# Attention results in two parts, no empty TensorE instructions in the first layer, and one more joined pair of steps

## The chip, the cores and the metric

The kernel runs on one core of a Trainium2 chip. The metric is the device time of one execution in microseconds, lower is better; the median of three executions of the kernel before is 538.77 us (537.64 to 538.97). Everything is computed in fp32.

## The reference

Two parts follow each other. The first is a linear attention with a decaying state (RWKV-6), for 4 batches, 8 heads, 768 tokens and head size 48:

```python
for t in range(S):
    cur = np.einsum('bhd,bhe->bhde', u[None] * kt, vt)
    y[:, :, t] = np.einsum('bhd,bhde->bhe', rt, state + cur)
    state = wt[:, :, :, None] * state + np.einsum('bhd,bhe->bhde', kt, vt)
```

The second is a two-layer network over the 3072 tokens, each a row of 8 x 48 = 384 numbers:

```python
h = x @ w_in            # (3072, 384) x (384, 2048), the first layer
g = h - np.tanh(h)
return g @ w_out        # (3072, 2048) x (2048, 384), the second layer
```

## The kernel before

**Blocks and steps.** The tokens are cut into eight blocks of 384 (a batch has two, `q` is 0 or 1). For each block the network runs through 16 steps `f`, one for each 128 columns of `w_in`. While block `i` goes through the network, the attention of block `i + 1` is worked out between its steps, so `xT`, the transposed input of the next block, is ready when it begins. All engine orders but that of POOL are fixed by the order in which the code is written: in each step the plan (`plan`) names the attention work, `ops` lists what VectorE does and in which order, and `due` holds the second-layer products of earlier steps with the step in which TensorE gets them (`add_due`).

**First layer.** `first` (L892) makes the 128 x 384 product `hp` of one step with three matmuls of 384 columns; each fp32 matmul is two hardware instructions in the trace, so a step is six. Behind each matmul stand 0, 2 or 3 empty instructions (`NO_OP`), as the table `SPACED` says for the block and the part of it. For some pairs of steps (`JOINED`) both products are made together by a scheme with fewer multiplications (`Twos.begin`, L939 to L970): eleven matmuls of 192 columns (22 instructions, L958) into the PSUM tiles `att0` and `att1`, with sums of weights (`kept`, formed by VectorE at the places of `FORMED`) and differences of token columns (`turned`, L942), and four VectorE additions afterwards (`joint`, L968).

**Activation and second layer.** ScalarE takes `tanh` twice (L984, L985) and a square (L988), VectorE multiplies them to `g` (L902). For most blocks the second layer uses a scheme with 15 products of 128 x 128 for two steps; VectorE forms sums of `g` for it (L1007), and TensorE makes the products in two parts of six (L1088, twelve instructions each, in step `f + 2` and `f + 3` of the odd step `f`) and one of three. In a joined pair the sums of an odd step are made one step later than otherwise (`carried`).

**Attention results.** `together` (L755) makes the block's `y`, transposed, in `att0` and `att1`. For each of 8 heads and 6 chunks of 64 tokens there is one product from the states (`pre` with `states`; with `q` = 0 the first chunk has none) and one from the scores (`v` with `scores`), each 48 x 64 and small enough that four run in different quarters of the array. They come in four stretches of 48 instructions (two parts, two halves `cross` each). An empty GpSimd memset between the first and the second stretch of the same half keeps their order. With `q` = 1 the states come first, with `q` = 0 the scores. Behind them ScalarE copies the result to `xT` (L753), and small DMAs of SyncE fill its holes (L801). This happens in step 13 of blocks 0 and 1 and in step 12 of blocks 2 to 6, after the second-layer products that are due in that step. The scores of the current chunk are written into `scores` by VectorE before (`diagonal_in`, L407: one copy for pairs 2 and 3, then one for pairs 0 and 1).

Of the kernel before, what the change touches and what calls it, by code (L numbers as in the profile page):

```python
# [50 lines left out]
B, H, S, D = 4, 8, 768, 48  # L51
P = 128
L = 64
NB = 384
NQ = S // NB
NCH = NB // L
NCP = NCH // 2
# [4 lines left out]
UP = 2  # L62
HALVES = (UP, 0)
ALL = tuple(range(NPAIR))
# [15 lines left out]
LATE = 3  # L80
SPACED = (3, 0), (0, 3), (3, 2), (2, 3), (3, 2), (2, 3), (3, 0), (0, 0)

# [38 lines left out]
TWOS = range(7)  # L121
BESIDE = (1, 3, 4, 7)
JOINED = {2: (4, 7), 3: BESIDE, 4: BESIDE, 5: BESIDE, 6: BESIDE, 7: TWOS}
PAIRS = range(1, 2), range(3, 5), range(7, 8)
LEFT = range(0, 3, 2), range(5, 7)
FORMED = {(1, 8): (1, (0, 2, 1, 4, 3)), (1, 15): (0, (0, 2, 1, 4, 3)), (2, 6): (2, (0, 2, 1, 4, 3)),
          (6, 11): (3, (0, 2)), (6, 12): (4, (0, 2)), (6, 13): (3, (1, 4, 3)), (6, 14): (4, (1, 4, 3))}
# [8 lines left out]
def kernel(  # L136
# [193 lines left out]
    class Block:  # L330
# [425 lines left out]
        def together(self, ps):  # L756

            self.results(ps)
            yp, spread, St, ended = self.yp, isinstance(ps, Kept), states[self.q], {}

            def scores(p, c, h, par):
                toks = slice(64 * par, 64 * par + 64)
                return self.v[toks, c, p * D2 + h * D:p * D2 + (h + 1) * D], A[toks, h, p, c, :]

            def from_state(p, c, h, par):
                rows = slice(64 * h, 64 * h + D)
                return St[rows, p, 2 * c + par, 0:D], self.chunk("pre", p, 2 * c + par, spread)[rows]

            def stretch(of, cross):
                first = cross not in ended  # L770
                begun = set()
                for n in range(UP):
                    for c in range(NCP):
                        for h in range(2):
                            for x in range(2):
                                p, par = UP * n + x, x ^ cross
                                if of is from_state and not (self.q or c or par):
                                    continue
                                lhs, rhs = of(p, c, h, par)
                                e0, n0 = 64 * (h ^ x), (n * NCP + c) * L  # L780
                                done = nc.tensor.matmul(yp[x][e0:e0 + D, par, n0:n0 + L], lhsT=lhs, rhs=rhs,  # L781
                                                        start=first and (x, e0) not in begun, stop=True,
                                                        skip_group_check=True)
                                begun.add((x, e0))
                                if not first and len(begun) == 1:
                                    begin_behind(ended[cross], done)
                if first:
                    ended[cross] = nc.gpsimd.memset(ended_at, 0.0)
                    begin_behind(done, ended[cross])

            for of in (from_state, scores) if self.q else (scores, from_state):
                for cross in range(2):
                    stretch(of, cross)
            self.result_out(ALL, None if spread else [nc.scalar.copy] * 2)
            self.fill_holes([nc.sync])

# [95 lines left out]

    def first(xT, f, hp, apart=0):
        for kc in reversed(range(KC)):
            nc.tensor.matmul(hp, lhsT=w_in_sb[:, f, kc, :], rhs=xT[kc],  # L895
                             start=(kc == KC - 1), stop=(kc == 0))
            for _ in range(apart):
                nc.tensor.nop(nofuse=True, hint="apart")
        return hp
# [448 lines left out]
    for i, blk in enumerate(blocks):  # L1348
# [9 lines left out]
        for f in range(NF):  # L1358
# [6 lines left out]
            if not joined:  # L1365
                h = first(here, f, to[:, 0:NB], SPACED[i][f > 12 + (i < 2)])
                g, made, square, later_ops = slight(h, now, i, f)
            elif f % 2 == 0:
                for op in behind:
                    op()  # L1370
                behind = []
                outs = twos.begin(ps_a, f // 2)
                if near:
                    for name in ("split 2 0", "split 2 1", "split 0 01"):
                        later.phase(ps_a, name)
# [25 lines left out]
            if (i, f) in FORMED:  # L1401
                spare += twos.weight_forms(*FORMED[i, f])
            if later and i in JOINED and f == (i == 2) or i == blocks_n - 2 and f == 14:
                spare += twos.token_forms(xT if f > 1 else here, twos.halves((turned, 0), (turned, NB)))
# [206 lines left out]
```

## Time and profile before

| | |
|---|---|
| median of three executions | 538.77 us |
| the profiled execution's own time | 538.27 us |
| its span, first to last instruction | 536.4 us |
| mean granted TensorE clock | 0.995 |
| TensorE busy (PE) | 526.9 us, 98% |
| VectorE busy (DVE) | 462.5 us, 86% |
| ScalarE busy (ACT) | 310.3 us, 58% |
| GpSimd busy (POOL) | 9.1 us, 2% |

A row of a timeline gives the start in us from the span's start, the length, the engine, the line, the operation with the tiles it writes and reads, and how many instructions were merged. Matmuls overlap: the length of a row reaches to the end of its last instruction, and the time that a row takes from the stream is the start of the next row less its own.

### The profile page before, as it was taken

The numbers are of one execution on the slowest core, as the hardware profiler recorded it, in microseconds if no ns is written. First come the engines' busy times: TensorE is split into PE (matmuls) and PEld (weight loads), VectorE is DVE, ScalarE is ACT, GpSimd is POOL, SyncE is SP. The second block draws the span as 40 slices with busy tenths as digits, with TensorE's granted clock in tenths as the row PEclk, the third lists the DMA queues.
The fourth block names the chain that finished last, engine by engine and source line by source line (L and its number), as shares of the span: only waits on it lengthen the run. The fifth ranks groups of instructions, "written<-read, shape, count | busy, mean of one in ns | idle before, by whom it ended". The sixth has DMA issues, their size and how long they took to land.

```text
span 536.4 us, 14922 instructions
## 1 busy us (share of the span) xinstructions
PE 526.9 (98%) x5950; PEld 437.5 (82%) x5950; DVE 462.5 (86%) x970; ACT 310.3 (58%) x720; POOL 9.1 (2%) x57
## 2 busy tenths in 40 slices
PE   8899999999999999999999999999999999999996
PEld 5756666677887889889789898899888897899994
DVE  7899897699979889988998899988999889667874
ACT  4899984666445573555655475374735655435450
POOL 1100000000000000000000000000000000000001
PEclk9899999999999999999999999999999999999999
DMA  8698733252302622162313722146221510100011
GB/s 280 224 404 333 241 105 109 89 148 61 120 13 89 163 74 89 51 137 82 120 57 75 178 60 68 50 90 165 63 90 39 140 40 2 56 1 2 11 34 47
DMA packets 53046, 56.33 MB, mean 105 GB/s; under 512 B 21488, under 2 KB 50928, under 8 KB 52976
## 3 DMA queue, kind: packets, MB, share of 16 engines
q1 hardware_dynamic: 52592, 55.18, 34.2%
q8 instruction: 49, 0.80, 0.7%
q14 instruction: 21, 0.17, 0.1%
q10 hardware_dynamic: 288, 0.10, 0.1%
q0 software_dynamic: 96, 0.07, 0.1%
HBM read 44.73 MB, written 4.72 MB: 92 GB/s over the span
## 4 chain that ended last, share of the span: by engine, by line
PE 96%; DMA 1%; issue 1%; ACT 0%; DVE 0%; SPq 0%; PEldq 0%; PEld 0%; DVEq 0%
PE acc L1088 27%; PE hp L895 27%; PE att L958 17%; PE acc L1039 6%; PE att L781 4%; PE hp L1088 3%; PE att L1088 3%; PE att L504 3%; PE att L585 2%; PE acc L1066 1%; PE att L895 1%; DMA r<-in_rT 1%; PE acc L895 1%; PE att L527 1%; PE att L689 1%
## 5 line engine op out<-in xcount | busy, mean ns | idle before, releaser
L895 PE MATMUL hp<-xT,w_sb 128*128 128x384 f32 x438 | 154.3, 488 | 0.7 <-issue 0.7
L1088 PE MATMUL acc<-forms,g 128*128 128x128 f32 x972 | 135.9, 276 | 0.0
L1088 PEld LDWEIGHTS acc<-forms,g 128*128 128x128 f32 x972 | 124.0, 192 | 4.3
L895 PEld LDWEIGHTS hp<-xT,w_sb 128*128 128x128 f32 x438 | 78.6, 190 | 43.5 <-issue 0.9
L1007 DVE TENSOR_TENSOR g<-g 128x256 f32<-128x256 f32 x270 | 107.1, 419 | 4.6 <-PE acc L1088 0.3
L984 ACT ACTIVATE h<-hp 128x384 f32<-128x384 f32 x73 | 35.9, 492 | 96.8 <-PE hp L895 96.8
L902 DVE SCALAR_TENSOR_TENSOR g<-h,qa 128x384 f32<-128x384 f32 x112 | 61.7, 551 | 21.8 <-ACT h L988 21.4
L988 ACT ACTIVATE h<-h 128x384 f32<-128x384 f32 x113 | 58.7, 519 | 0.0
L1088 PE MATMUL acc<-w_sb,g 128*128 128x128 f32 x324 | 54.1, 276 | 0.0
L958 PE MATMUL att<-xT,w_sb 128*128 128x192 f32 x250 | 53.0, 326 | 0.0
L1088 PEld LDWEIGHTS acc<-w_sb,g 128*128 128x128 f32 x324 | 46.4, 192 | 5.5
L968 DVE TENSOR_TENSOR joint<-joint,att 128x384 f32<-128x384 f32 (+1 forms) x72 | 34.6, 501 | 18.0 <-PE att L958 11.0
L984 ACT ACTIVATE h<-joint 128x384 f32<-128x384 f32 x36 | 18.7, 518 | 39.7 <-DVE joint L968 39.7
L958 PEld LDWEIGHTS att<-xT,w_sb 128*128 128x128 f32 x250 | 41.4, 190 | 0.0
L985 ACT ACTIVATE qa<-hp 128x384 f32<-128x384 f32 x73 | 35.7, 489 | 0.0
L1123 DVE TENSOR_TENSOR sums<-sums 128x256 f32<-128x256 f32 x84 | 32.9, 410 | 1.4 <-ACT sums L1100 0.9
L1039 PE MATMUL acc<-w_sb,sums 128*128 128x384 f32 x96 | 33.7, 487 | 0.0
L271 ACT ACTIVATE up<-raw 128x768 f16<-128x768 f32 (+1 forms) x32 | 32.7, 1093 | 0.0
L1039 PEld LDWEIGHTS acc<-w_sb,sums 128*128 128x128 f32 x96 | 18.1, 190 | 12.3
L427 DVE TENSOR_TENSOR_SCAN pre<-w,start 128x780 f32<-128x780 f32 x14 | 25.0, 1782 | 0.8
L439 DVE TENSOR_TENSOR_SCAN post<-w,seed 128x780 f32<-128x780 f32 x14 | 24.9, 1775 | 0.0
L958 PE MATMUL att<-turned,kept 128*128 128x192 f32 x126 | 23.9, 326 | 0.0
(157 smaller groups left out, 768.3 us busy)
## 6 DMA issues: line engine op xcount, KB each, us to landing
raw<-in_weights SPq DMA_DIRECT2D x16, 768.0 KB, 6.4
w<-in_wT SPq DMA_DIRECT2D x7, 780.0 KB, 5.4
k<-in_kT SPq DMA_DIRECT2D x7, 768.0 KB, 4.5
r<-in_rT SPq DMA_DIRECT2D x7, 768.0 KB, 4.4
v_sb<-in_v SPq DMA_DIRECT2D x8, 576.0 KB, 4.1
k<-in_tokens SPq DMA_DIRECT2D x7, 576.0 KB, 4.2
r<-in_tokens SPq DMA_DIRECT2D x7, 576.0 KB, 4.9
out_y<-sums SPq DMA_DIRECT2D x18, 128.0 KB, 1.9
```

The source lines that it names most:

```text
L271: return lambda: nc.scalar.activation(out=to, in_=of, func=AF.Copy, scale=scale, bias=bias)
L895: nc.tensor.matmul(hp, lhsT=w_in_sb[:, f, kc, :], rhs=xT[kc], start=(kc == KC - 1), stop=(kc == 0))
L902: return lambda: nc.vector.scalar_tensor_tensor(out=out, in0=in0, scalar=scalar, in1=in1, op0=op0, op1=ALU.mult)
L958: nc.tensor.matmul(to, lhsT=lhs, rhs=rhs, start=n == 0, stop=n + 1 == len(of))
L968: return [lambda of=of: nc.vector.tensor_tensor(out=of[0], in0=of[1], in1=of[2], op=ALU.add) for of in ((h[:, 0:5:4], twice(h[:, 3]), both ...
L984: made = nc.scalar.activation(out=t, in_=h, func=AF.Tanh, scale=INNER / UPSCALE)
L985: nc.scalar.activation(out=by, in_=h, func=AF.Tanh, scale=OUTER / UPSCALE)
L988: nc.scalar.activation(out=t, in_=t, func=AF.Square, accum_out=top[:, n:n + 1])
L1007: return lambda: nc.vector.tensor_tensor(out=G[:, to:to + 2], in0=two(G, g_at(q, a0), g_at(q, a1)), in1=two(G, g_at(q, b0), g_at(q, b1)), ...
L1039: nc.tensor.matmul(acc, lhsT=g[:, j * P:(j + 1) * P], rhs=w_out_sb[:, f, :], start=(f == self.first), stop=(f == NF - 1))
L1088: nc.tensor.matmul(to, lhsT=G[:, g_at(q, a), :], rhs=rhs, start=start, stop=stop, skip_group_check=True)
L1123: ops.append(lambda op=op, at=at: nc.vector.tensor_tensor(out=at[0], in0=at[1], in1=at[2], op=OPS[op]))
```

## The change

Three edits stand in it. The table `SPACED` and the argument `apart` go, so `first` issues no empty instruction any more; of 516 empty instructions of TensorE 33 are left, all in the second layer of block 0. `together` is cut into `of_scores` and `of_states`, the scores always first; in the loop over steps the products that are due (`add_due`) now stand between the two. In block 2, pair 1 (steps 2 and 3) becomes a joined pair; for that the sums of weights for pair 1 are formed first (block 1, step 8), those for pairs 3 and 4 last (block 2, step 6), the token differences of block 2 are made in step 0 and not in step 1, and the early `split` of the attention's keys stays out of block 2.

```diff
-SPACED = (3, 0), (0, 3), (3, 2), (2, 3), (3, 2), (2, 3), (3, 0), (0, 0)
...
-JOINED = {2: (4, 7), 3: BESIDE, 4: BESIDE, 5: BESIDE, 6: BESIDE, 7: TWOS}
+JOINED = {2: (1, 4, 7), 3: BESIDE, 4: BESIDE, 5: BESIDE, 6: BESIDE, 7: TWOS}
...
-FORMED = {(1, 8): (1, (0, 2, 1, 4, 3)), (1, 15): (0, (0, 2, 1, 4, 3)), (2, 6): (2, (0, 2, 1, 4, 3)),
+FORMED = {(1, 8): (0, (0, 2, 1, 4, 3)), (1, 15): (2, (0, 2, 1, 4, 3)), (2, 6): (1, (0, 2, 1, 4, 3)),
...
         def together(self, ps):
 
+            self.of_scores(ps)
+            self.of_states()
+
+        def of_scores(self, ps):
+
             self.results(ps)
-            yp, spread, St, ended = self.yp, isinstance(ps, Kept), states[self.q], {}
+            self.spread, self.stretched = isinstance(ps, Kept), {}
+            for cross in range(2):
+                self.stretch(0, cross)
+
+        def of_states(self):
+            for cross in range(2):
+                self.stretch(1, cross)
+            self.result_out(ALL, None if self.spread else [nc.scalar.copy] * 2)
+            self.fill_holes([nc.sync])
...
-    def first(xT, f, hp, apart=0):
+    def first(xT, f, hp):
         for kc in reversed(range(KC)):
             nc.tensor.matmul(hp, lhsT=w_in_sb[:, f, kc, :], rhs=xT[kc],
                              start=(kc == KC - 1), stop=(kc == 0))
-            for _ in range(apart):
-                nc.tensor.nop(nofuse=True, hint="apart")
         return hp
...
-                if near:
+                if near and i > 2:
                     for name in ("split 2 0", "split 2 1", "split 0 01"):
                         later.phase(ps_a, name)
...
-            if later and i in JOINED and f == (i == 2) or i == blocks_n - 2 and f == 14:
+            if later and i in JOINED and not f or i == blocks_n - 2 and f == 14:
...
+            if later and "results" in phases.get(f, ()):
+                later.of_scores(ps_a)
             add_due(now)
             if later and "results" in phases.get(f, ()):
-                later.together(ps_a)
+                later.of_states()
```

The first place is TensorE at the results of the next block, here in step 12 of block 2. Before, the due products stand ahead of both parts:

```order
L895 MATMUL hp<-xT_1315,w_sb 128x384
L898 NO_OP x3
L1088 MATMUL acc_131<-forms,g 128x128 x4
L1088 MATMUL acc_602<-w_sb,g 128x128
L1088 MATMUL acc_602<-forms,g 128x128
L781 MATMUL att_126<-pre,states_103 48x64
L781 MATMUL att_125<-pre,states_103 48x64
```

Now the 48 matmuls with the scores (the last two are shown) stand directly behind the first layer's, then the due products, then the 48 with the states:

```order
L795 MATMUL att_126<-scores,v_sb 48x64
L795 MATMUL att_125<-scores,v_sb 48x64
L1094 MATMUL acc_131<-forms,g 128x128 x4
L1094 MATMUL acc_602<-w_sb,g 128x128
L1094 MATMUL acc_602<-forms,g 128x128
L795 MATMUL att_126<-pre,states_103 48x64
L795 MATMUL att_125<-pre,states_103 48x64
```

The scores have moved ahead of one part of six second-layer products, and one run of 96 small matmuls has become two of 48.

The second place is VectorE in steps 2 to 4 of block 2, around the new joined pair. Before (`pre<-w,start` is the scan for the next block's attention, `g<-h,qa` the activation's product, `g<-g` the sums for the second layer):

```order
L427 SCALAR_TENSOR_TENSOR pre<-w,start 128x780
L1007 TENSOR_TENSOR g<-g 128x256
L902 SCALAR_TENSOR_TENSOR g<-h,qa 128x384
L1007 TENSOR_TENSOR g<-g 128x256 x4
L426 RECIPROCAL start<-whole 128x12
```

Now, from the first of the two scans on:

```order
L426 SCALAR_TENSOR_TENSOR pre<-w,start 128x780
L974 TENSOR_TENSOR joint<-joint,att_126 128x2x192
L1013 TENSOR_TENSOR g<-g 128x256
L974 TENSOR_TENSOR joint<-joint,att_125 128x384
L974 TENSOR_TENSOR joint<-joint,att_125 128x192
L974 TENSOR_TENSOR joint<-joint,att_125 128x384
L1013 TENSOR_TENSOR g<-g 128x256
L425 RECIPROCAL start<-whole 128x12
L426 SCALAR_TENSOR_TENSOR pre<-w,start 128x780
L908 SCALAR_TENSOR_TENSOR g<-h,qa 128x384
L1013 TENSOR_TENSOR g<-g 128x256
L908 SCALAR_TENSOR_TENSOR g<-h,qa 128x384
```

Four additions have come in, and both products `g<-h,qa` of the pair now stand behind the second scan; the three sums `g<-g` of step 4, two of which TensorE reads in that step, follow the last row shown.

The third place is ScalarE in the same steps, now:

```order
L965 COPY joint<-att_126 128x192
L1106 ACTIVATE sums<-acc_602 128x512
L1106 ACTIVATE sums<-acc_131 128x512
L990 ACTIVATE h<-joint 128x384
L991 ACTIVATE qa<-joint 128x384
L994 ACTIVATE h,top<-h 128x384
L990 ACTIVATE h<-joint 128x384
L991 ACTIVATE qa<-joint 128x384
L994 ACTIVATE h,top<-h 128x384
```

Before, these activations read `hp` and not `joint`, and the first three stood ahead of the two `sums<-acc`, which wait for the last products of the block before.

More of the change, by code (lines that the diff above doesn't have):

```diff
@@ L756, in together, with stretch @@
         def together(self, ps):
+            self.of_scores(ps)
+            self.of_states()
+        def of_scores(self, ps):
             self.results(ps)
-            yp, spread, St, ended = self.yp, isinstance(ps, Kept), states[self.q], {}
+            self.spread, self.stretched = isinstance(ps, Kept), {}
[6 more added lines that the diff above has]
+            self.fill_holes([nc.sync])
+        def stretch(self, part, cross):
+            yp, spread, St, ended = self.yp, self.spread, states[self.q], self.stretched
             def scores(p, c, h, par):
@@ L767, in from_state @@
                 return St[rows, p, 2 * c + par, 0:D], self.chunk("pre", p, 2 * c + par, spread)[rows]
[L769 to L795, printed above, removed]
+            of, first, begun, last = (from_state if part else scores), cross not in ended, set(), None
+            for n in range(UP):
+                for c in range(NCP):
+                    for h in range(2):
+                        for x in range(2):
+                            p, par = UP * n + x, x ^ cross
+                            if part and not (self.q or c or par):
+                                continue
+                            lhs, rhs = of(p, c, h, par)
+                            e0, n0 = 64 * (h ^ x), (n * NCP + c) * L
+                            last = nc.tensor.matmul(yp[x][e0:e0 + D, par, n0:n0 + L], lhsT=lhs, rhs=rhs,
+                                                    start=first and (x, e0) not in begun, stop=True,
+                                                    skip_group_check=True)
+                            begun.add((x, e0))
+                            if not first and len(begun) == 1:
+                                begin_behind(ended[cross], last)
@@ L797, in fill_holes @@
+            if first:
+                ended[cross] = nc.gpsimd.memset(ended_at, 0.0)
+                begin_behind(last, ended[cross])
         def fill_holes(self, engines, which=range(2 * KC)):
@@ L1365 @@
             if not joined:
-                h = first(here, f, to[:, 0:NB], SPACED[i][f > 12 + (i < 2)])
+                h = first(here, f, to[:, 0:NB])
                 g, made, square, later_ops = slight(h, now, i, f)
```

## The prediction

> **What bounds the kernel now.** I read the page first: busy times, granted clock and the chain that ended last.
>
> ```profile
> span 536.4 us, 14922 instructions
> PE 526.9 (98%) x5950; PEld 437.5 (82%) x5950; DVE 462.5 (86%) x970; ACT 310.3 (58%) x720; POOL 9.1 (2%) x57
> PEclk9899999999999999999999999999999999999999
> PE 96%; DMA 1%; issue 1%; ACT 0%; DVE 0%; SPq 0%; PEldq 0%; PEld 0%; DVEq 0%
> ```
>
> TensorE (PE) is busy 98% of the span, the chain is PE for 96%, and its clock is full from the third slice on. Whether it ever waits for others is in the view of the waits, PE alone (us in total, times, longest):
>
> ```profile
> PE att L504 <- issue: 1.5, 1, 1.5
> PE hp L895 <- issue: 0.7, 1, 0.7
> ```
>
> Beside two short waits at the very start these are all, and both are for "issue", for nothing that another engine does. The 1.5 lies in the first 25 us, which no edit touches. So the kernel is one row of TensorE instructions without holes, and the forecast is the sum of what the change does to that row: instructions saved, changes of form added, waits that come in and the one that goes. VectorE at 86% and the ScalarE chain count where they come late.
>
> **Empty instructions.** Timeline of PE, first in block 1, where the table gives none, then in block 2, with three behind each matmul (a row's time is the next row's start less its own):
>
> ```profile
> 107.20 2.10 PE L895 MATMUL hp<-xT,w_sb 128*128 128x384 f32 x6
> 109.14 0.61 PE L1088 MATMUL acc<-w_sb,g 128*128 128x128 f32 x4
> ...
> 161.27 2.10 PE L895 MATMUL hp<-xT,w_sb 128*128 128x384 f32 x6
> 163.21 1.05 PE L1088 MATMUL acc<-forms,g 128*128 128x128 f32 x8
> ...
> 164.55 2.10 PE L895 MATMUL hp<-xT,w_sb 128*128 128x384 f32 x6
> ```
>
> A step takes 1.94 us without them and 1.94 with nine. The 483 that go were hidden behind running matmuls, and the clock was full with and without them: 0 us. (The twelve second-layer instructions after the second step take 164.55 - 163.21 = 1.34; I need that below.)
>
> **Splitting the results.** A run of small matmuls costs something at both ends. Block 2, then a small run between two large ones, with the end of a third in block 3:
>
> ```profile
> 171.10 2.10 PE L895 MATMUL hp<-xT,w_sb 128*128 128x384 f32 x6
> 173.13 1.63 PE L504 MATMUL att<-pre,post 48*64 48x64 f32 x96
> ...
> 201.52 1.05 PE L1088 MATMUL acc<-forms,g 128*128 128x128 f32 x8
> ...
> 202.95 1.56 PE L781 MATMUL att<-pre,states 48*48 48x64 f32 x96
> 204.33 1.52 PE L781 MATMUL att<-scores,v_sb 64*48 64x64 f32 x96
> 205.78 2.20 PE L895 MATMUL hp<-xT,w_sb 128*128 128x384 f32 x6
> ```
>
> ```profile
> 224.65 1.14 PE L958 MATMUL att<-xT,w_sb 128*128 128x192 f32 x6
> ...
> 228.22 1.05 PE L1088 MATMUL acc<-forms,g 128*128 128x128 f32 x8
> ...
> 230.96 2.10 PE L895 MATMUL hp<-xT,w_sb 128*128 128x384 f32 x6
> 232.99 1.63 PE L504 MATMUL att<-pre,post 48*64 48x64 f32 x96
> 234.55 1.16 PE L1088 MATMUL acc<-forms,g 128*128 128x128 f32 x8
> ...
> 235.99 1.46 PE L895 MATMUL hp<-xT,w_sb 128*128 128x384 f32 x4
> ```
>
> Going in: six of L895 ahead of small ones take 173.13 - 171.10 = 2.03 and not 1.94, so 0.09. Coming out: twelve of L1088 behind small ones take 235.99 - 234.55 = 1.44 and not 1.34, so 0.10. Inside the run there is a fixed part too, since the array fills and empties. Instructions of L781 in two stretches of that run (us, PE busy, count):
>
> ```profile
> 202.95:203.25 0.30, 0.30 (x20) 1.00 0.01 0
> 202.95:205.25 2.30, 2.30 (x164) 1.00 0.04 7
> ```
>
> 144 more in 2.00 us are 13.9 ns each; 192 would take 2.67 and took 205.78 - 202.95 = 2.83, so 0.16 is fixed. From below: the half with the way out takes 1.45, the half with the way in 1.38, at least 0.07. From above: two lone runs like L504's (234.55 - 232.99 = 1.56) would take 3.12, 0.29 more. I take 0.16, as it comes from these instructions themselves. Each split adds one run: 0.16 + 0.09 + 0.10 = 0.35 us (0.26 to 0.48). Seven blocks (0 to 6) prepare a next one: **+2.45 us** (1.8 to 3.4). The twelve second-layer instructions are only moved. Where the states came first, their sums now have more time.
>
> **Block 0: the scores are asked for too early.** Here the scores came second (q of block 1 is 1). PE, then DVE:
>
> ```profile
> 76.34 2.10 PE L1039 MATMUL acc<-w_sb,sums 128*128 128x384 f32 x6
> 78.37 1.56 PE L781 MATMUL att<-pre,states 48*48 48x64 f32 x96
> ```
>
> ```profile
> 75.15 1.95 DVE L407 COPY_PREDICATED scores<-mask_all,diagonal 128x768 f32<-128x768 uint8 x2
> ```
>
> The second of the two copies, for pairs 0 and 1, with which the stretch begins, ends at 77.10. PE would start the scores at 76.34 + 0.09 = 76.43; the due products and the states had covered that. No edit touches DVE's rows before. PE waits 77.10 - 76.43 = 0.67 and some hundredths for the release: **+0.70 us** (0.6 to 0.75). Behind the waiting matmul stand the six of L1039 and the states, so all of PE.
>
> **Pair 1 of block 2.** Two steps of 1.94 are 3.88; a joined pair is 228.22 - 224.65 = 3.57: **-0.31 us**. But with it two of the three sums for the pair before (steps 0 and 1) come a step later on DVE, behind the pair's own products. Block 3 has the same pair, and there ACT (first row) and DVE run so:
>
> ```profile
> 229.76 1.09 ACT L1100 ACTIVATE sums<-acc 128x512 f32<-128x512 f32 x2 [0.46 <-PE acc L1088]
> ```
>
> ```profile
> 228.42 1.41 DVE L968 TENSOR_TENSOR joint<-joint,att 128x384 f32<-128x384 f32 x3 [1.03 <-PE att L958]
> ...
> 233.53 0.56 DVE L902 SCALAR_TENSOR_TENSOR g<-h,qa 128x384 f32<-128x384 f32 x1 [0.22 <-ACT h L988]
> 234.00 1.09 DVE L1007 TENSOR_TENSOR g<-g 128x256 f32<-128x256 f32 x3
> 235.01 0.76 DVE L1123 TENSOR_TENSOR sums<-sums 128x256 f32<-128x256 f32 x2
> ```
>
> ```profile
> L1007 DVE TENSOR_TENSOR g<-g 128x256 f32<-128x256 f32 x270 | 107.1, 419 | 4.6 <-PE acc L1088 0.3
> L427 DVE TENSOR_TENSOR_SCAN pre<-w,start 128x780 f32<-128x780 f32 x14 | 25.0, 1782 | 0.8
> ```
>
> PE's products end, ACT takes two `sums` and six activations, DVE the product (released by ACT) and three sums `g` (0.42 each, three in 1.09), ready at 234.42, 234.76 and 235.09. PE needs the first for its third product of step 4 and the last for the fifth. In block 3 that fits, because 96 small matmuls (L504) stand ahead of these products. In block 2 they come a step later. On block 3's clock: after the pair 24 products end at 230.96, the step takes 1.94, so the products begin at 232.90 and the third is due 4 x 0.112 (1.34 / 12) later, at 233.35. It waits for 234.42 + 0.05: 1.12. The fifth is then due at 234.92 and waits for 235.14: 0.22. Together **+1.34 us**. Block 2's DVE has the second scan and its reciprocal (0.2, an estimate) there: through by 228.42 + 1.41 + 0.42 + 0.2 + 1.78 = 232.2, before the two products, so ACT stays the last. If the sums were earlier, the next would be late: DVE's `pre` for the run L504 of step 5 would be ready at 235.01 + 0.76 + 1.75 = 237.52, by this row of block 2,
>
> ```profile
> 170.83 1.75 DVE L446 TENSOR_TENSOR pre<-r,pre 128x1536 f32<-128x1536 f32 x1
> ```
>
> while PE without the first wait gets there at 232.90 + 1.34 + 2.03 = 236.27: 1.25 instead of 1.34. So 1.1 to 1.5.
>
> **The issue wait in block 6.** It stands right behind the results:
>
> ```profile
> 457.01 0.59 PE L895 MATMUL hp<-xT,w_sb 128*128 128x384 f32 x1
> 458.25 1.77 PE L895 MATMUL hp<-xT,w_sb 128*128 128x384 f32 x5 [0.66 <-issue]
> ```
>
> ```profile
> q8 instruction: 49, 0.80, 0.7%
> ```
>
> After small matmuls the first takes 0.32 + 0.10, so the next was due at 457.43 and came 0.82 late. The queue that brings instructions moved 49 packets of 0.80 MB / 49 = 16 KB; PE has 5950 + 5950 + 516 instructions, 253 a packet. The results are 384 (192 matmuls, as many loads) in 2.83 us, one and a half packets: I read the wait as the next packet's. A half is 192, less than one packet, and then come 24 in 1.34 us. So it goes: **-0.82 us** (0 if it only moves, -1.5 if untraced runs pay the longer of the two issue waits here).
>
> The Trainium skill ("Runtime: NRT & Kernel Launch", section Instruction fetch mechanics) has blocks of 16 KiB and 256 instructions, which the 49 packets agree with. It also says that a block's crossing is mostly hidden, since the sequencer, at about 20 cycles an instruction, is slower than the fill. That the trace doesn't bear out here: a small matmul and its load follow each other in 13.9 ns, and PE stood 0.82 us with no other releaser. By the page nothing would come back, and the sum would be 4.18.
>
> **Sum.** 2.45 + 0.70 + 1.34 - 0.31 - 0.82 = +3.36 us. The profiled execution took 538.27, with 1.9 around its span; that gives 541.6. The median of the runs lies 0.5 above it, which gives 542.1. I take 541.9. What a measurement of this kernel tells from no change is about 0.3%, 1.6 us.
>
> **Rivals.**
> - *The two DVE waits don't come.* PE is later by the splits, DVE has holes, and block 3 does the same pair without a wait. Against it: the chain in block 2 starts with PE's own products, and in block 0 DVE's rows follow without a hole. If DVE is 0.7 and 1.3 us earlier there: 538.77 + 2.45 - 0.31 - 0.82 = 540.1, within 0.3%.
> - *The issue wait stays or moves.* For it: the instruction addresses shift by 483, and other runs of 192 may meet a late packet. Against it: the runs of L504 (192 with their loads) had none after the start. 538.77 + 4.18 = 542.95, slower.
> - *The scores wait in blocks 2 to 6 as well.* They write the tiles that DVE's last read of the update leaves:
>
> ```profile
> 201.12 0.35 DVE L597 TENSOR_TENSOR states<-states,att 128x192 f32<-128x192 f32 x1
> ```
>
> It ends at 201.47, and PE comes at 201.52 + 0.09. If DVE is 0.3 later than I think: 5 x 0.3 more, 543.6.
> - *Instruction fetch costs far more in untraced runs.* The place is the long run in each of seven blocks, the price between the two issue waits, 0.82 and 1.5, so 5.7 to 10.5 us, all of which the split would save. In the middle: 538.77 + 4.18 - 8.1 = 534.9, faster. It decides from 5.8 us on (4.18 + 1.6). Against it: the traced run paid 0.82 and took only 0.5 less than the median.
>
> **How the numbers follow.** My forecast 0.66; waits don't come 0.12; issue wait stays 0.10; more waits 0.05; fetch 0.07. Slower 0.66 + 0.10 + 0.05 = 0.81, same 0.12, faster 0.07. The likeliest's own range, from the terms' bounds: 1.8 + 0.6 + 1.1 - 0.31 - 1.5 = 1.7 to 3.4 + 0.75 + 1.5 - 0.31 = 5.3 at the extremes; all at one end at once is unlikely, so +2.3 to +4.6, 540.8 to 543.1. The range takes in the stayed wait and most of the first rival: 539.7 to 543.3.
>
> **What would show it.** The split: seven pairs of small runs, each 1.49 or so, with 2.03 before and 1.44 after. Block 0: a PE wait of 0.7 at the scores, released by DVE's `scores`. Block 2: waits of 1.1 and 0.2 in step 4's products, released by `g`. No PE wait for issue after 25 us. L895 rows still 1.94. The forecast is wrong if the small halves cost less than 0.07 at their ends, if block 2's step 4 starts without a wait, or if the time without the profile moves by something that the trace doesn't show.

## The result, and the profile after

The changed kernel takes 541.32 us (median of 5 runs, 540.86 to 542.12) where the kernel before takes 538.77 (537.64 to 539.45): a ratio of 1.0051, 95% interval 1.0035 to 1.0067, so 1.9 to 3.6 us slower. A second comparison gave 1.0051 again (after_again, below). The forecast was 541.9, in 539.7 to 543.3.

The page of the changed kernel, to be laid beside the one of before (busy times, the chain that ended last, the queue of the instructions):

```profile
span 539.3 us, 14456 instructions
PE 529.9 (98%) x5960; PEld 438.7 (81%) x5960; DVE 464.3 (86%) x974; ACT 310.3 (58%) x721; POOL 9.1 (2%) x57
PE 92%; DVE 3%; DMA 1%; issue 1%; ACT 1%; PEld 0%; SPq 0%; PEldq 0%; DVEq 0%
q8 instruction: 48, 0.79, 0.6%
```

VectorE has entered the chain with 3%. The view of PE's waits says where (us in total, times, longest):

```profile
PE att L318 <- POOL ident masks.py:199: 2.1, 1, 2.1
PE acc L1094 <- DVE g L1013: 1.0, 1, 1.0
PE att L795 <- DVE scores L406: 0.6, 1, 0.6
PE acc L903 <- DMA xT<-late: 0.4, 1, 0.4
```

The first and the last lie in the first 26 us. The other two are the waits forecast for block 2 and block 0, and no wait for issue is left in the list. PE in block 0, at the results:

```profile
72.95 2.10 PE L903 MATMUL hp<-xT,w_sb 128*128 128x384 f32 x6
75.68 1.56 PE L795 MATMUL att<-scores,v_sb 64*48 64x64 f32 x96 [0.64 <-DVE scores L406]
77.17 2.20 PE L1045 MATMUL acc<-w_sb,sums 128*128 128x384 f32 x6
79.30 1.56 PE L795 MATMUL att<-pre,states 48*48 48x64 f32 x96
80.80 2.20 PE L903 MATMUL hp<-xT,w_sb 128*128 128x384 f32 x6
```

The scores would have begun at 72.95 + 2.03 = 74.98 and begin at 75.68: 0.70. PE in block 2, first the products of step 4 behind the new joined pair, then the results:

```profile
169.55 0.61 PE L1094 MATMUL acc<-forms,g 128*128 128x128 f32 x4
171.13 0.71 PE L1094 MATMUL acc<-forms,g 128*128 128x128 f32 x4 [0.97 <-DVE g L1013]
171.80 0.49 PE L1094 MATMUL acc<-w_sb,g 128*128 128x128 f32 x2
...
172.35 2.10 PE L903 MATMUL hp<-xT,w_sb 128*128 128x384 f32 x6
174.38 1.63 PE L503 MATMUL att<-pre,post 48*64 48x64 f32 x96
...
200.83 2.10 PE L903 MATMUL hp<-xT,w_sb 128*128 128x384 f32 x6
202.86 1.56 PE L795 MATMUL att<-scores,v_sb 64*48 64x64 f32 x96
204.35 1.16 PE L1094 MATMUL acc<-forms,g 128*128 128x128 f32 x8
...
205.88 1.56 PE L795 MATMUL att<-pre,states 48*48 48x64 f32 x96
207.37 2.20 PE L903 MATMUL hp<-xT,w_sb 128*128 128x384 f32 x6
```

The twelve products of step 4 take 172.35 - 169.55 = 2.80, and undisturbed ones take 1.34, so 1.46 is lost there (the forecast's two waits came to 1.34). The split: 2.03 ahead, halves of 1.49, 1.53 between, all as forecast.

What the page does not list are holes too small for it. In block 4 the second half takes 333.96 - 332.17 = 1.79 and not 1.49, in block 5 1.79 and not 1.41 (80 instructions), in block 6 1.57:

```profile
332.17 1.86 PE L795 MATMUL att<-pre,states 48*48 48x64 f32 x96
333.96 0.59 PE L903 MATMUL hp<-xT,w_sb 128*128 128x384 f32 x1
```

Together 0.30 + 0.38 + 0.08 = 0.76, and block 1 has 0.10 of the same kind. The forecast had none of this.

**The account by blocks.** All profiles can be laid over each other at the same instructions: the first second-layer matmul of block 0 (33.16 us from the start in the first profile of before, 31.70 in that of after), then the first matmul behind the results of each block. The table gives how much longer than in the first profile of before each stretch was, in us; "start" is the time up to block 0's first second-layer matmul, "end" what comes after block 6's results up to the last matmul (there before has its wait of 0.82; behind that matmul each profile has another 5.0 to 6.5). The names are those of the experiments.

| | start | 0 | 1 | 2 | 3 | 4 | 5 | 6 | end |
|---|---|---|---|---|---|---|---|---|---|
| after | -1.46 | 1.05 | 0.43 | 1.57 | 0.33 | 0.65 | 0.71 | 0.43 | -0.82 |
| after_again | -0.54 | 1.04 | 0.33 | 1.57 | 0.33 | 0.46 | 0.43 | 0.34 | -0.82 |
| after_r_later | -0.05 | 1.05 | 0.33 | 1.57 | 0.33 | 0.34 | 0.33 | 0.41 | -0.82 |
| block0_states | -0.49 | 0.34 | 0.33 | 1.56 | 0.33 | 0.50 | 0.69 | 0.34 | -0.82 |
| pair1_apart | -1.82 | 1.29 | 0.33 | 0.35 | 0.33 | 0.39 | 0.33 | 0.35 | -0.82 |
| split_alone | -1.99 | 1.16 | 0.33 | 1.16 | 0.33 | 0.35 | 0.33 | 0.34 | -0.82 |
| whole_results | -1.30 | 4.06 | 1.58 | 1.23 | 0.00 | 0.63 | 0.21 | 1.55 | -0.81 |
| no_empty | -1.15 | 5.29 | 1.31 | 0.00 | 0.00 | 0.42 | 0.54 | 1.37 | -0.82 |
| lead200 | 12.54 | 0.00 | 0.00 | 0.98 | 0.86 | 0.62 | 0.00 | 0.00 | -0.81 |
| before_again | -1.64 | 0.00 | 0.00 | 0.89 | 0.00 | 0.00 | 0.00 | 0.00 | 0.27 |
| block6_two | -1.61 | 0.00 | 0.00 | 0.85 | 0.00 | 0.00 | 0.00 | 0.00 | -0.81 |
| boot_shift | -0.06 | 0.00 | 0.00 | 0.77 | 0.00 | 0.00 | 0.00 | 0.00 | -0.81 |
| r_later | -2.12 | 0.00 | 0.00 | 0.00 | 0.00 | 0.00 | 0.00 | 0.00 | -0.81 |

Stretches without an edit agree to some thousandths of a microsecond; what varies from run to run is the start (31.0 to 33.2 us, lead200 apart) and the small holes. Of block 0's 5.29 in no_empty, 1.2 is a wait for a converted weight (VectorE's `w_sb`, at 35.3) that belongs to the start; 0.24 of pair1_apart's 1.29 was lost in one first-layer step (at 55.5 of its profile), and the cause is open.

### The profile page after: what moved, and what is told of

It is laid out like the page before. It is cut to its first block, busy times and chain, and to the rows that moved or that the text cites. A ratio compares the mean times of both kernels' runs of the same rounds, so it can differ in the third digit from the quotient of the medians.

```text
span 539.3 us, 14456 instructions
## 1 busy us (share of the span) xinstructions
PE 529.9 (98%) x5960; PEld 438.7 (81%) x5960; DVE 464.3 (86%) x974; ACT 310.3 (58%) x721; POOL 9.1 (2%) x57
## 4 chain that ended last, share of the span: by engine, by line
PE 92%; DVE 3%; DMA 1%; issue 1%; ACT 1%; PEld 0%; SPq 0%; PEldq 0%; DVEq 0%
PE acc L1094 27%; PE hp L903 25%; PE att L964 17%; PE acc L1045 5%; PE att L795 4%; PE hp L1094 3%; PE att L1094 3%; PE att L503 2%; PE att L584 2%; PE acc L1072 1%; PE att L903 1%; DMA xT<-late 1%; DVE scores L511 1%; DVE post L438 1%; PE acc L903 1%
## 5 line engine op out<-in xcount | busy, mean ns | idle before, releaser
L903 PE MATMUL hp<-xT,w_sb 128*128 128x384 f32 x426 | 150.0, 488 | 0.0
L903 PEld LDWEIGHTS hp<-xT,w_sb 128*128 128x128 f32 x426 | 76.6, 191 | 41.6
L964 PE MATMUL att<-xT,w_sb 128*128 128x192 f32 x260 | 55.1, 326 | 0.0
L974 DVE TENSOR_TENSOR joint<-joint,att 128x384 f32<-128x384 f32 (+1 forms) x76 | 36.5, 501 | 19.7 <-PE att L964 12.9
L964 PEld LDWEIGHTS att<-xT,w_sb 128*128 128x128 f32 x260 | 43.1, 191 | 0.0
L964 PE MATMUL att<-turned,kept 128*128 128x192 f32 x132 | 25.0, 326 | 0.0
```

What stands on the lines that cost most here:

```text
L964: nc.tensor.matmul(to, lhsT=lhs, rhs=rhs, start=n == 0, stop=n + 1 == len(of))
L974: return [lambda of=of: nc.vector.tensor_tensor(out=of[0], in0=of[1], in1=of[2], op=ALU.add) for of in ((h[:, 0:5:4], twice(h[:, 3]), both ...
```

## The experiments

My theory was that of the forecast: the sum of splits, two VectorE waits, a joined pair and a packet of instructions that no longer comes late, with the empty instructions worth nothing. The rivals: the packet's wait has another cause, or moves; the empty instructions do something.

**no_empty** and **lead200** touch nothing but empty instructions. The first is the kernel before with the table emptied:

```diff
-SPACED = (3, 0), (0, 3), (3, 2), (2, 3), (3, 2), (2, 3), (3, 0), (0, 0)
+SPACED = ((0, 0),) * 8
```

> The kernel before, only without the 483 empty instructions of the first layer. By my theory an empty instruction takes no time but sets where PE's instruction packets of 16 KB (256 instructions) begin, and PE waits where a run of 192 small matmuls meets a late packet. Counted from the trace of before (a packet is asked for when PE is about 115 to 140 instructions into the one before, and is usable 1.1 + 1.1 + 1.4 us later), packets would come late in block 0's results and in block 6's, 1.4 us each, in place of 0.8 in block 6: +2.0, about 540.8. Steps of the first layer still take 1.94. Rival: the empty instructions do nothing at all, and block 6 keeps its wait: 538.8. Rival: the empty instructions kept something (clock, or weights loads) apart, and the steps get longer than 1.94.

Measured: 545.54 against 539.04, ratio 1.0125 (1.0097 to 1.0154). So removing instructions that take no time where they stand costs 6.5 us. The steps of the first layer still take 1.94; the loss is in the results and right behind them. PE at block 0's:

```profile
80.09 1.19 PE L781 MATMUL att<-scores,v_sb 64*48 64x64 f32 x68
84.32 1.09 PE L781 MATMUL att<-scores,v_sb 64*48 64x64 f32 x28 [3.04 <-issue]
85.34 3.19 PE L895 MATMUL hp<-xT,w_sb 128*128 128x384 f32 x6
88.37 2.10 PE L1039 MATMUL acc<-w_sb,sums 128*128 128x384 f32 x6
```

PE stands 3.04 us in the middle of a run whose operands are all there. The instruction queue's packet was sent at 81.96, took 1.01, and PE went on 1.35 after its end. The same stretch by windows (busy time and count of PE, PEld, DVE, ACT, POOL; then PE's granted clock, the DMA share, GB/s):

```profile
80.00:82.00 2.00, 1.28 (x88) 1.13 (x77) 2.00 (x5) 0.00 (x0) 0.09 (x1) 1.00 0.97 340
82.00:84.00 2.00, 0.00 (x0) 0.00 (x0) 1.97 (x4) 0.00 (x0) 0.00 (x0) 0.99 0.08 28
84.00:85.00 1.00, 0.68 (x26) 0.68 (x28) 0.40 (x1) 0.00 (x0) 0.00 (x0) 0.50 0.00 0
```

Two things I had not counted. The DMA engines are full (0.97) until 82, and the packet leaves when they come free. And at 84.0, after 2.7 us without work (from 80.09 + 1.19 = 81.28), the granted clock falls to 0.50, and the next six matmuls of L895 take 88.37 - 85.34 = 3.03 in place of 2.04. The windows of 1 us that follow have 0.50, 0.50 and 0.82, so half the clock lasts from 84.0 to about 87.4, 3.4 us. The Trainium skill ("TensorE: Matmul & The Clock Gate", section Part 1: The HAM clock gate) says that the array goes to half its clock after an idle window and back after a busy one, of about 3.4 us. The trace agrees in the 0.50 and in the 3.4 at half clock; but here a wait of 3.04 was enough, and the fall came 2.7 us into it. The waits come where the count of the packets put them: the one in block 6 as large as expected (1.37 by the table, 1.4 expected), the one in block 0 larger (3.04 in place of 1.4). And there are holes of 0.3 to 0.5 in blocks 1, 4 and 5 (block 1's 1.31 has the slow matmuls just named in it).

The second puts 200 empty instructions ahead of everything:

```diff
+        for _ in range(200):
+            nc.tensor.nop(nofuse=True, hint="ahead")
         blk.tiles["w"] = states0
```

> The kernel before with 200 empty TensorE instructions ahead of its first matmul, where PE waits 2.1 us for GpSimd anyway. Nothing else moves but the place of every 256th instruction. By the theory of the packets no run of small matmuls meets a late one any more: the wait in block 6 goes (-0.8), and the long issue wait in the first 25 us too, as far as data doesn't keep PE there (0 to -1.5): 536.5 to 538.0, with no wait for issue in the list. If the packets are not the cause: 538.8 or, should 200 empty instructions last longer than the 2.1 us, more.

Measured: 551.86, ratio 1.0246 (1.0218 to 1.0274). A miss, and an instructive one. Its waits:

```profile
PE att L319 <- issue: 15.9, 1, 15.9
PE att L781 <- issue: 1.8, 3, 0.8
PE att L689 <- issue: 1.0, 1, 1.0
```

The first matmul starts at 15.91 and not at 2.08: an empty instruction is not free where nothing runs over it. The first of the 200 starts at 1.02 in the trace, so one takes (15.91 - 1.02) / 200 = 0.074 us on average; most follow each other at 0.07. Three of them are some 0.22 us, behind a matmul of 0.65 (two instructions of 0.323): hidden, as forecast. And the wait of block 6 did go (-0.81 at the end), but blocks 2, 3 and 4 got one each. So what moves the packets moves the waits: the packets are the cause. The traces have a stricter sign of it. Number PE's matmuls, weight loads and empty instructions in the order in which they start. Every gap of over 0.12 us between two instructions of the results, and the two waits right behind them in block 6 of the unchanged kernel (21 cases in ten profiles), stand at the 2217th, 3492nd, 5023rd, 5279th, 6810th, 7829th, 8341st, 9360th, 10890th or 11403rd, each to within one place. Any two of these lie a whole multiple of about 255 apart (to within three), a packet's length, whichever kernel it is. My count of where a late one would fall was too simple, since it gave every packet the same delay.

**whole_results** is the changed kernel with the results undivided, behind the due products, in the old order:

```diff
-            if later and "results" in phases.get(f, ()):
-                later.of_scores(ps_a)
             add_due(now)
             if later and "results" in phases.get(f, ()):
-                later.of_states()
+                later.together(ps_a)
```

> The changed kernel with one edit undone: scores and states of the results stand together again, behind the due products, in the old order (no empty instructions, pair 1 of block 2 joined). By my prediction's steps the split costs 2.45 and block 0's wait 0.70, so this would be 541.3 - 3.15 = 538.2, plus what the packets cost: by the count for the kernel without empty instructions 1.4 each in blocks 0 and 6, so 541.0. Without a cost of the packets: 538.2. It keeps the waits of 1.2 and 0.2 in block 2.

Measured: 545.83, ratio 1.0152 (1.0121 to 1.0183), far over the 541.0 expected. So the split, for which I had 3.15 us of cost, makes this kernel some 4 us faster. The waits:

```profile
PE att L800 <- issue: 4.8, 3, 3.1
```

In the table it pays 4.06 in block 0 where the changed kernel pays 1.05, and 1.55 in block 6 against 0.43. My reading, from the rows alone, is that behind a half run of 192 instructions come slow ones, in which a late packet costs less than in a whole run of 384.

**pair1_apart** is the changed kernel with pair 1 of block 2 separate:

```diff
-JOINED = {2: (1, 4, 7), 3: BESIDE, 4: BESIDE, 5: BESIDE, 6: BESIDE, 7: TWOS}
+JOINED = {2: (4, 7), 3: BESIDE, 4: BESIDE, 5: BESIDE, 6: BESIDE, 7: TWOS}
```

(with the order in `FORMED`, the step of the token differences and the early `split` as before).

> The changed kernel with one edit undone: pair 1 of block 2 is two separate steps again. By the trace of after the joined pair saves 0.31 and brings waits of 1.45 in step 4's products: -1.14, about 540.2, and no wait for g in the list. If another wait stands behind the one that goes (VectorE's pre for the small matmuls of step 5): 541.3, with that wait in its place. All small halves of the results stay at 1.49, but where 256 instructions end shifts by 12, so that a hole of up to 0.4 may come or go in blocks 4 to 6.

Measured: 541.4 in 12 runs, ratio 1.0050 (1.0031 to 1.0069), by the time of whole runs not to be told from the changed kernel's 1.0051. The trace tells them apart: block 2 costs 0.35 and not 1.57, the wait for `g` is out of the list, and no other has taken its place. So the joined pair costs 1.22 there. The holes in blocks 4 to 6 are down to 0.06 at most, with packets that begin elsewhere.

**split_alone**, the kernel before with the split as its only edit; **block6_two**, with two empty instructions in block 6 (`(3, 0)` of `SPACED` becomes `(2, 0)` there); **boot_shift**, with packets shifted from the start (`spare=94, ahead=5` becomes `spare=64, ahead=7`, `(3, 0)` for block 0 becomes `(4, 0)`); and **before_again**, unchanged, ran together.

> The kernel before with one edit alone: the results in two parts, scores first, the due products between. The empty instructions stay, and pair 1 of block 2 stays apart. By my prediction's steps: +2.45 for seven splits (0.33 to 0.35 each by the trace of after) + 0.70 for block 0's scores - 0.82 for block 6's packet = +2.3, about 541.1, in the trace 1.05 more by the end of block 0's results and 0.34 more by each later one. Rival: a half run is short enough for a late packet to hide behind the products, and the split pays as much as it costs: within 0.5 of 538.8. Rival: halves meet late packets that the whole did not: holes of up to 0.4 in blocks 4 and 5, 541.8.

> The kernel before with two instead of three empty instructions behind each first-layer matmul of block 6 (21 fewer, so the instructions behind them stand 21 places earlier in their packets). By the theory of the packets the one wait for issue after the start (0.8 at 457) goes, since the packet is asked for 1.9 us earlier before its need; nothing else moves: 538.0 where the kernel before has 538.8. If that wait was not the packet's: 538.8 with the wait in its place. Should a packet in block 7 come late instead, it would be seen as a new wait for issue.

> The kernel before with the packets shifted from the start: 28 of its first 94 tiny matmuls without use are left out (30 out, 2 long ones in, 56 instructions fewer in all), and block 0 gets four empty instructions behind each matmul in place of three (42 more), so that the later blocks stand only 14 places from where they were. By the count of the packets the long wait for issue in the first 25 us goes (1.5 in the trace of before), the one in block 6 too (0.8), and with the first the dip of the granted clock at 22 to 26 us (0.57 there): 535.7 to 537.0, and a mean clock of 0.998 to 1.0 in most runs. Rival: the dip has another cause and comes in as many runs as before: 538.0. Rival: fewer tiny matmuls at the start let the clock fall there: over 539.

> The kernel before, unchanged, for a second look at its first 25 us. If the long wait for issue there (1.5) comes from a packet of instructions that waits behind data, it varies with the run: a run with mean clock 1.0 should have no such wait and no dip, and end 2 us earlier than the first profile; a run at 0.995 should have both. The wait of 0.8 in block 6 is there in either case, since no data moves then.

*before_again* (537.75, one run) gave what the others are to be read by:

```profile
PE hp L895 <- issue: 0.9, 1, 0.9
PE att L781 <- issue: 0.6, 1, 0.6
```

The wait in block 6 is there, longer (1.09 by the table), and there is one in block 2 that the first profile lacks. PE there, and the windows around it:

```profile
201.31 1.56 PE L781 MATMUL att<-pre,states 48*48 48x64 f32 x96
202.70 0.27 PE L781 MATMUL att<-scores,v_sb 64*48 64x64 f32 x3
203.56 1.55 PE L781 MATMUL att<-scores,v_sb 64*48 64x64 f32 x93 [0.59 <-issue]
```

```profile
193.50:197.00 3.50, 3.50 (x22) 2.71 (x22) 3.50 (x10) 2.46 (x7) 0.00 (x0) 1.00 0.75 225
197.00:198.25 1.25, 1.25 (x11) 1.14 (x11) 1.22 (x5) 1.18 (x4) 0.00 (x0) 1.00 0.00 0
198.25:201.25 3.00, 3.00 (x18) 2.26 (x16) 2.83 (x7) 1.17 (x3) 0.00 (x0) 1.00 0.95 261
```

Two loads (of `k` and of `r`, 768 KB each) fill the engines with a gap of 1.25 us between. In the first profile of before the packet went out in that gap, at 198.62 (196.98 on this profile's clock, whose start is 1.64 shorter); here it was sent at 201.18, 4.2 us later, when the second load had drained, was in by 202.13, and PE went on 1.43 after that. The start has neither the issue wait of 1.5 nor a granted clock below 0.9 (the first profile's second slice of 40 has 0.8).

*block6_two* (537.91 against 538.18, ratio 0.9985, 0.9971 to 0.9999) loses exactly the wait of block 6 and nothing else; the one in block 2 is there as in before_again. *boot_shift* (540.45, ratio 1.0047, 1.0030 to 1.0065) failed: it loses block 6's wait, but the start has other issue waits in its stead (1.5 and 0.7) and is 1.6 us longer than in before_again, and the mean clock was below 0.998 in most of its runs. The time is that of its last rival, that fewer tiny matmuls let the clock fall; its one profile, with a full clock at the start, doesn't show whether that is the reason. Where the packets fall at the start I can't place by counting, as the loads of the weights keep the DMA engines full there. *split_alone* (539.97, ratio 1.0035, 1.0021 to 1.0049) has 0.33 to 0.35 in blocks 1 and 3 to 6, 1.16 in block 0 and the packet's 0.8 in block 2; its 1.8 us are less than the 2.3 expected, but inside the interval's 1.1 to 2.6. The rival that a split pays for itself is out while the empty instructions stand.

**block0_states** turns the halves round in block 0 alone:

```diff
-                later.of_scores(ps_a)
+                later.of_scores(ps_a, int(not i))
...
-                later.of_states()
+                later.of_states(int(bool(i)))
```

> The changed kernel with one thing turned round: in block 0 alone the half with the states comes first, the due products next, the scores last. The split stays (+0.35), the wait for VectorE's scores (0.70) should go, as the due products and the states cover it again: by the end of block 0's results 0.7 less than in the trace of after, 540.6. Rival: the states are late instead (their sums are VectorE's too), and a wait of the same size stands there: 541.3.

**after_again** is the changed kernel, unchanged:

> The changed kernel, unchanged, beside the others and for a second trace. The waits in block 0 (0.70) and block 2 (1.2 and 0.2) come from the order of VectorE's work and return within 0.05. The holes of 0.2 to 0.4 in the second halves of blocks 4 and 5 are late packets, by my reading ones that waited for a load of data to drain, and may come, go or stand in another block. 541.3; by its first 25 us 1.0 more or less.

PE in block 0 of block0_states:

```profile
73.92 2.10 PE L903 MATMUL hp<-xT,w_sb 128*128 128x384 f32 x6
75.94 1.56 PE L795 MATMUL att<-pre,states 48*48 48x64 f32 x96
77.44 2.20 PE L1045 MATMUL acc<-w_sb,sums 128*128 128x384 f32 x6
79.57 1.56 PE L795 MATMUL att<-scores,v_sb 64*48 64x64 f32 x96
```

No wait stands at either half, and block 0 costs 0.34: the 0.70 was the price of asking for the scores first. In whole runs (541.05, ratio 1.0045, 1.0029 to 1.0061, against 541.25, 1.0051, 1.0035 to 1.0066) 0.7 us is too little to be told. after_again has the waits in block 0 and 2 back to a hundredth, and smaller holes (0.12 and 0.10 in blocks 4 and 5, none in block 6). At its start (19.8) stands a wait for issue of 1.8 us, and the granted clock stays full behind it; so a wait of that length does not by itself bring the dip that the first profile of before has there.

**after_r_later** and **r_later** move a load. In both `11: ["r"]` becomes `13: ["r"]` in the table of loads, in the first for blocks 2 to 6 of the changed kernel, in the second for block 2 of block6_two.

> The changed kernel with the load of r issued in step 13 in place of step 11 in blocks 2 to 6 (TensorE's, VectorE's and ScalarE's rows stay the same). If packets that wait for this load to drain make the holes in the second halves of blocks 4 and 5 (0.30 and 0.38 in the first trace, 0.12 and 0.10 in the second), both halves take 1.49 and 1.41 there, and only block 6, where no load stands, may keep up to 0.1. Waits in block 0 and block 2 stay (0.7, 1.2, 0.2). 541.0. Rival: the holes stay, so the load has nothing to do with them: 541.3.

> The kernel before with two empty instructions in block 6 in place of three, and with one load (r for the block after next, 768 KB) issued in step 13 of block 2 and not in step 11. By the reading that a packet of instructions waits until a load has drained, the wait of 0.5 to 0.9 for issue in block 2's results goes, since no load then stands before its packet: no wait for issue at all after 25 us, and 0.3 to 0.7 less than the kernel with the empty instructions alone: 537.4. Rival: the packet is late for another reason and the wait stays: 537.9. Rival: the load, now behind six stores of the output, comes late for block 3: a wait of VectorE for r, and more than 538.

*after_r_later*: the hole of block 4 is gone, with the engines idle ahead of it where the changed kernel had them at 0.92. The windows of the changed kernel, then those of after_r_later, then its PE:

```profile
327.50:330.50 3.00, 3.00 (x102) 2.06 (x100) 2.86 (x6) 1.25 (x4) 0.09 (x1) 1.00 0.92 268
```

```profile
327.50:330.50 3.00, 3.00 (x20) 1.93 (x20) 2.79 (x9) 1.16 (x4) 0.00 (x0) 1.00 0.01 3
333.48 1.56 PE L795 MATMUL att<-pre,states 48*48 48x64 f32 x96
334.97 1.24 PE L903 MATMUL hp<-xT,w_sb 128*128 128x384 f32 x3
```

334.97 - 333.48 = 1.49. Blocks 4 and 5 cost 0.34 and 0.33, block 6, where no load stands, keeps 0.07. That bears out the reading of the holes, in one profile; the unchanged kernel's second one had only 0.12 and 0.10 to lose. The time (541.59, ratio 1.0059, 1.0043 to 1.0076) doesn't show it; the start of 31 to 33 us hides it.

*r_later*: 535.94 against 538.26, ratio 0.9960 (0.9945 to 0.9975), faster than both kernels. Its list of PE's waits is complete with

```profile
PE att L319 <- POOL ident masks.py:199: 2.1, 1, 2.1
PE att L504 <- ACT k L464: 0.7, 1, 0.7
```

and both are in the first 10 us: no wait for issue anywhere, and PE busy 99% of the span:

```profile
span 533.5 us, 14905 instructions
PE 525.5 (99%) x5950; PEld 436.6 (82%) x5950; DVE 462.6 (87%) x970; ACT 310.3 (58%) x720; POOL 9.1 (2%) x57
```

Its kernel differs from block6_two's in this one load, and block 2 loses the 0.85 that block6_two has there. The two waits (0.8 to 1.1 and 0.9) account for 1.7 to 2.0 of the 2.3 won, and the interval (1.4 to 3.0) takes that in; the start of its profile is the shortest of all, and whether that is the edit's doing or the run's is not settled. One thing doesn't fit a packet that only waits for loads: here it left 1.72 us ahead of block 2's results, with the engines idle for 2 us, where the first profile of before had sent it 4.33 ahead. So when a packet is asked for varies as well, and why is open.

## Why the prediction was right, and where it was not

**The sum** came out: +3.36 forecast, and the cleanest comparison, after_r_later against the first profile of before, whose starts differ by 0.05, gives +3.54 from block 0 on (1.05 + 0.33 + 1.57 + 0.33 + 0.34 + 0.33 + 0.41 - 0.82). It has the load moved; the two profiles of the changed kernel itself give +4.35 and +3.68 by the same sum, with the holes that the forecast had at nothing. The medians give 2.55, 3.0 and, with the load moved, 3.35. In the first profile the start stands between these traces and the time (-1.46): that "no edit touches" it was true, but it isn't the same from run to run (31.5 and 33.2 us in two profiles of the kernel before), so a sum of traces is known only to about 1 us in the time of a run.

**The split, +2.45.** Measured 0.33 to 0.35 in each undisturbed block, 2.35 in seven. Right to 0.1, with its parts: 0.09 in, 0.10 out, 0.15 in the run (2 x 1.49 - 2.83).

**Block 0, +0.70.** Measured 0.70 (1.05 less 0.35), released by VectorE's scores; it goes when the states come first. Right, with the mechanism shown.

**Pair 1, -0.31 + 1.34.** Measured +1.22 net by the pair with and without. The waits themselves were 1.13 and 0.12 (forecast 1.12 and 0.22); what was mis-sized is the restart: after each wait the second matmul follows 0.21 and not 0.11 behind the first, 0.10 lost twice. The chain was the forecast's, with VectorE nearer to it than I had it:

```profile
168.85 0.56 DVE L908 SCALAR_TENSOR_TENSOR g<-h,qa 128x384 f32<-128x384 f32 x1
...
170.18 0.56 DVE L908 SCALAR_TENSOR_TENSOR g<-h,qa 128x384 f32<-128x384 f32 x1 [0.31 <-ACT h L994]
```

It waits for ScalarE only 0.31 before the product. Whether the run L504 would be late next, had the sums been earlier (1.25), wasn't tried.

**The issue wait, -0.82.** "So it goes" holds for block 6 (-0.82, with 0 to 0.09 left in its second half). But it moved too, as the rival had it: 0.30 + 0.38 in blocks 4 and 5 in the first trace, 0.12 + 0.10 in the second. Its cause, PE's packets of instructions, is shown by three kernels that differ from the one before in empty instructions alone (no_empty, lead200, block6_two).

**Empty instructions, 0.** This step failed as it was argued. They take no time where they stand, and the step of 1.94 is the same, as forecast. But they are also what places the packets, and without them, and with nothing else changed, the kernel loses 6.5 us. I priced the removal and the split one by one against the same kernel, in which hardly a run met a late packet. One after the other they are: the removal +6.5 (no_empty), with pair 1 joined as well +6.8 (whole_results), and with the split on top +2.6, so the split, taken last, is worth -4.2. The means were there: the working counted 253 instructions to a packet, but used the count for one wait, and didn't ask where the other packets would begin once 483 instructions are gone. In the other order the removal costs little: the split alone costs 1.8 (split_alone), and with the empty instructions gone as well it is 2.4 (pair1_apart), a difference within the two intervals. So 0 holds behind the split and is 6.5 wrong without it. The forecast had argued only for block 6 that a half is shorter than a packet; that the halves would also take up the late packets which the removal brings to the other blocks was no step of it, and in that the number was lucky.

The Trainium skill's rule that I weighed ("Runtime: NRT & Kernel Launch", section Instruction fetch mechanics), that a crossing of 16 KiB is mostly hidden, doesn't hold for runs of small matmuls here: PE stood 0.5 to 3.1 us for issue at one crossing, and at every such place it went on 1.2 to 1.6 us after the packet's end.

**The rivals.** That the VectorE waits don't come: out. More waits on the tile `att` in blocks 2 to 6: none. Fetch far dearer in runs without a profile: no sign of it; the kernel that loses all such waits gains 2.3, not 8.

## What to carry to other kernels

TensorE was fed packets of some 255 instructions here, so an instruction that takes no time still moves every packet behind it. The price of adding or removing any is read from where the next packets fall, above all in runs of small matmuls like these (13.9 ns for a matmul and its load). A wait for "issue" in such a run is to be looked up in the queue of the instructions and in the DMA share of the 3 us before it; where a load stands there, the load can be moved. And edits that touch one resource are to be priced in sequence, not each alone against the kernel before.

## What the runs showed of the hardware

- **A packet of instructions is held back by a load of data.** In block 2 of the kernel before it was sent in the gap between two loads in one profile and 4.2 us later, behind the second, in the other. In blocks 4 and 5 of the changed kernel it was sent 1.31 and 1.51 us after the first half's beginning, each time as a load ended, and with that load moved 0.81 and 1.02 after it: half a microsecond earlier, and the holes of 0.30 and 0.38 were gone. It need not wait for the load's very end: in block 4 of after_again it left after 1.07, with the last packets of the load still moving.
- **An empty TensorE instruction takes 0.074 us** when nothing runs over it (200 in 14.9), and none when three stand behind matmuls of 0.65.
- **PE standing for 3.04 us halved its clock** for some 3.4 us, which cost another 1.0 in the six matmuls behind the run (no_empty; in whole_results a wait of 3.1 did the same).
- **A wait costs 0.10 more than its length** among 128 x 128 matmuls, since the one behind it follows at 0.21 in place of 0.11.
